# The second expert product as seven block products with transposed output, weights folded for four batches, and sums of weights kept in DRAM

## The chip, the cores and the metric

The kernel runs on one NeuronCore of a Trainium2 chip. The metric is the device time of one execution in microseconds. A core has TensorE (PE, with its weight loads as PEld), VectorE (DVE), ScalarE (ACT), GpSimd (POOL) and SyncE (SP), which issues the DMAs here. PE writes PSUM, which has eight banks of 512 float32 per partition; POOL works on SBUF alone.

## What is computed

Two attentions and a mixture of four experts (sizes: 8 batches, 8 heads, 576 tokens of 64; 32 packing queries; width 512, hidden width 1024):

```python
def sm_attn(qq, kk, vv):
    s = scale * np.matmul(qq, kk.transpose(0, 1, 3, 2))
    s = s - np.max(s, axis=-1, keepdims=True)
    a = np.exp(s)
    a = a / (np.sum(a, axis=-1, keepdims=True) + 1e-09)
    return np.matmul(a, vv)
p_packed = sm_attn(p, k, v)
out = sm_attn(q, p_packed, p_packed)
...
p = domain_probs / (domain_probs.sum(-1, keepdims=True) + 1e-09)
for e in range(E):
    h = np.maximum(x @ w1[e], 0.0)
    out += p[:, e:e + 1] * (h @ w2[e])
```

Here x holds the attention's output, one row for each of the 4608 tokens.

## The kernel before

**Folded first product.** The second attention's output is a product of token weights (32 per head) with packed values. So x @ w1 is computed as (token weights) @ (packed values @ w1). The inner factor is called G: for each head, 32 rows by the hidden width.

**Three products for one.** Operands of the large products are split into a high part, rounded to float32r, and a low part, the remainder. Each product is three TensorE products: high by low, high by high, low by high. `split` (L70 to L75) makes the parts: the high one with a cast, mostly on ACT, the low one with a subtraction, mostly on POOL.

**Tiling and loops.** Batches go in pairs: four superbatches of 1152 tokens. The hidden width of each expert is cut in two, so there are eight chunks (expert, half) for a superbatch, 32 in all. A chunk has these steps:
- `load_w1`, `load_w2`: loads 256 KB tiles (`wraw`) and splits them, anew for each superbatch.
- `g_stage` (L256): eight products of 512 columns, one for each head, for both batches; ACT copies the cross terms (L263), DVE adds them into `gs` (L265), ACT and DVE split the sum into `gh` and `gl`.
- `mm1` (L312): 16 groups of six products of 288 columns; the result has the hidden index on partitions and tokens along the free axis. ACT takes the relu as the high part (L316), DVE makes the low part (L317).
- `mm2` (L331): nine groups of twelve products of 512 columns, tokens on partitions. DVE multiplies by the expert's weight for each token and accumulates (L339; L336 for the first chunk). In the last chunk the accumulators go out (L342).

**Attention.** `pack_unit` is the first attention for one batch and four heads: scores (L113), softmax, transposes (L141, L145), packed values (L151, L159). `tok_unit` is the second attention's weights: scores (L182), 32 by 32 transposes and softmax on DVE (L186 to L198), split into `xh` and `xl`. Four units of each kind stand ahead of the loop, for the first superbatch, in an order that is written out by hand (the `emit` lines). The others are generators that advance by a stage at every second group of `mm2`.

**What sets the order.** The code is written in one order and the framework places the instructions of each engine, by its own model of time, where they can go; each engine then runs its list strictly in that order and waits at semaphores. All DMAs are issued from SP's list. Six PSUM banks serve `ps_aux`, two serve `ps_o`.

## Time and profile before

| | us |
|---|---|
| median of three runs | 1379.92 |
| range of the runs | 1378.01 to 1380.5 |
| span of the profiled execution | 1375.6 |

The profile is of one execution. Engine times in it are busy times; several engines are busy at once. A row of groups gives line, engine, operation, the tiles it writes and reads, shape, count, then busy time in us, mean ns of one, and the idle time of the engine ahead of them with what ended it. Products on PE overlap, so the mean of one is longer than the distance from one start to the next. A row of the chain or the timeline begins with the start and the length in us. Where groups of the same line have different shapes, the rows are shown by form.

The busiest groups on the engines other than PE are POOL's low parts of w1 (L75, 340.9 us in 252 instructions), DVE's additions into `gs` (L265, 338.1 us in 496) and DVE's low parts of the hidden values (L317, 216.7 us in 504).

### The profile page before, as it was taken

Reading aid. Unit: us, or ns where it says so; the run is one execution under the profiler, and the core shown is the slowest. Engines: PE = TensorE matmul, PEld = TensorE weight load, DVE = VectorE, ACT = ScalarE, POOL = GpSimd, SP = SyncE. Lnnn points to the kernel's source line nnn. Section 1 sums busy time; section 2 is a strip of 40 time slices with the busy share of each in tenths; the row PEclk is TensorE's granted clock in tenths of the full one; section 3 lists DMA queues with packets and bytes.
Section 4 is the critical chain, followed back from the end, with each engine's and each line's share of the span. In section 5 each row is a group of like instructions: output and inputs, shape, how many; then the busy total and the mean of one; then the engine's idle time right before and its main releaser. Section 6 shows DMA issues by size and latency. Waiting matters only on the chain.

```text
span 1375.6 us, 21317 instructions
## 1 busy us (share of the span) xinstructions
PE 1346.0 (98%) x7800; PEld 1144.1 (83%) x7800; DVE 993.8 (72%) x1734; ACT 690.8 (50%) x1402; POOL 568.9 (41%) x512
## 2 busy tenths in 40 slices
PE   6799999999999999999999999999999999999998
PEld 3588888878888888887888888888888888888887
DVE  7777766788867767689776667778867776666773
ACT  4744454545545545454555455554555455545531
POOL 4643444534434524444433445344444333443410
PEclk9899999999999999999999999999999999999999
DMA  9312222322232222222133222121123121112101
GB/s 296 105 40 80 74 87 72 98 66 85 73 114 83 80 76 71 88 72 65 55 100 102 84 77 82 56 88 55 54 62 108 47 61 55 54 55 62 54 1 69
DMA packets 64184, 106.83 MB, mean 78 GB/s; under 512 B 6097, under 2 KB 24657, under 8 KB 64081
## 3 DMA queue, kind: packets, MB, share of 16 engines
q1 hardware_dynamic: 64080, 105.48, 25.2%
q8 instruction: 62, 1.02, 0.3%
q14 instruction: 42, 0.34, 0.1%
HBM read 96.02 MB, written 9.44 MB: 77 GB/s over the span
## 4 chain that ended last, share of the span: by engine, by line
PE 86%; DVE 8%; POOL 2%; DMA 2%; issue 1%; ACT 1%; SPq 0%; POOLq 0%; ACTq 0%; DVEq 0%
PE ops L331 51%; PE aux L312 29%; PE aux L256 4%; DVE gs L265 3%; DMA wraw<-in_w 1%; DVE acc L339 1%; POOL w1st L75 1%; DVE gl L75 1%; PE aux L113 1%; DVE a L186 1%; PE aux L151 1%; DVE m L188 1%; DVE a L189 1%; PE aux L141 0%; DMA pb<-in_dp 0%
## 5 line engine op out<-in xcount | busy, mean ns | idle before, releaser
L75 POOL TENSOR_TENSOR w1st<-wraw,w1st 64x512 fp32r<-64x512 f32 x252 | 340.9, 1353 | 665.1 <-ACT w1st L72 626.7
L331 PE MATMUL ops<-w2l,hh 128*128 128x512 f32 x1152 | 450.9, 393 | 5.6 <-DVE acc L339 5.1
L331 PE MATMUL ops<-w2h,hh 128*128 128x512 f32 x1152 | 450.5, 391 | 0.0
L331 PE MATMUL ops<-w2h,hl 128*128 128x512 f32 x1152 | 448.1, 391 | 0.0
L265 DVE TENSOR_TENSOR gs<-aux,cross 32x512 f32<-32x512 f32 x496 | 338.1, 682 | 31.5 <-ACT cross L263 18.3
L317 DVE SCALAR_TENSOR_TENSOR hl<-aux,hh 128x288 fp32r<-128x288 f32 x504 | 216.7, 454 | 151.8 <-ACT hh L316 151.6
L312 PE MATMUL aux<-xl,gh 128*128 128x288 f32 x1008 | 295.7, 297 | 3.0 <-POOL xl L75 2.7
L312 PE MATMUL aux<-xh,gh 128*128 128x288 f32 x1008 | 295.2, 296 | 0.0
L339 DVE SCALAR_TENSOR_TENSOR acc<-ops,pb,acc 128x512 f32<-128x512 f32 x252 | 187.8, 749 | 137.3 <-PE ops L331 133.6
L312 PE MATMUL aux<-xh,gl 128*128 128x288 f32 x1008 | 284.1, 296 | 0.0
L316 ACT ACTIVATE hh<-aux 128x288 fp32r<-128x288 f32 x504 | 192.3, 414 | 171.8 <-PE aux L312 166.9
L331 PEld LDWEIGHTS ops<-w2l,hh 128*128 128x128 f32 x1152 | 216.3, 188 | 49.5 <-DVE acc L339 6.9
L263 ACT COPY cross<-aux 64x512 f32<-64x512 f32 x248 | 142.7, 582 | 225.5 <-PE aux L256 107.8
L331 PEld LDWEIGHTS ops<-w2h,hl 128*128 128x128 f32 x1152 | 215.6, 188 | 45.4
L331 PEld LDWEIGHTS ops<-w2h,hh 128*128 128x128 f32 x1152 | 216.2, 188 | 40.9
L72 ACT CAST w1st<-wraw 64x512 fp32r<-64x512 f32 x256 | 158.3, 618 | 143.9 <-DMA wraw<-in_w 140.1
L312 PEld LDWEIGHTS aux<-xl,gh 128*128 128x128 f32 x1008 | 190.0, 189 | 10.2 <-POOL xl L75 3.0
L312 PEld LDWEIGHTS aux<-xh,gh 128*128 128x128 f32 x1008 | 190.0, 189 | 5.0
L312 PEld LDWEIGHTS aux<-xh,gl 128*128 128x128 f32 x1008 | 187.3, 188 | 3.4
L75 POOL TENSOR_TENSOR w2l<-wraw,w2h 128x512 fp32r<-128x512 f32 x124 | 157.3, 1299 | 62.3 <-ACT w2h L72 39.0
L75 DVE TENSOR_TENSOR gl<-gs,gh 128x512 fp32r<-128x512 f32 x124 | 100.2, 829 | 19.9 <-ACT gh L72 19.4
L72 ACT CAST w2h<-wraw 128x512 fp32r<-128x512 f32 x128 | 78.1, 630 | 27.1 <-PE ops L331 6.5
(74 smaller groups left out, 675.7 us busy)
## 6 DMA issues: line engine op xcount, KB each, us to landing
wraw<-in_w SPq DMA_DIRECT2D x256, 256.0 KB, 2.9
kt<-in_k SPq DMA_DIRECT2D x32, 288.0 KB, 3.3
kt<-in_q SPq DMA_DIRECT2D x16, 576.0 KB, 3.8
out<-acc SPq DMA_DIRECT2D x36, 256.0 KB, 2.0
vt<-in_v SPq DMA_DIRECT2D x16, 512.0 KB, 4.7
vt<-in_v SPq DMA_DIRECT2D x16, 64.0 KB, 4.4
pt<-in_p SPq DMA_DIRECT2D x8, 64.0 KB, 3.4
pb<-in_dp SPq DMA_DIRECT2D x1, 72.0 KB, 5.7
```

What stands on the lines that cost most here:

```text
L72: nc.scalar.copy(out=dst_hi, in_=src)
L75: lo_eng.tensor_tensor(out=dst_lo, in0=src, in1=dst_hi.bitcast(F32), op=ALU.subtract)
L113: nc.tensor.matmul(out=ps[j * 64:(j + 1) * 64, 0:HS], lhsT=pbd[bi][:, 2 * g + j, :], rhs=kt[:, j, c * HS:(c + 1) * HS], start=True, stop=True,
L151: nc.tensor.matmul(out=ps[h * NPK:(h + 1) * NPK, 0:D], lhsT=at[0:n, c, h * NPK:(h + 1) * NPK], rhs=vt[0:n, c, h * D:(h + 1) * D], start=c ...
L256: nc.tensor.matmul(out=ps, lhsT=st["pgs"][:, h // 2, h % 2].rearrange("p a n -> p (a n)"), rhs=wst[h], start=True, stop=True,)
L263: nc.scalar.copy(out=cross, in_=ps[64:P, :])
L265: nc.vector.tensor_tensor(out=gs[hs * NPK:(hs + 1) * NPK, bi, :], in0=ps[bi * NPK:(bi + 1) * NPK, :], in1=cross[bi * NPK:(bi + 1) * NPK, : ...
L312: nc.tensor.matmul(out=ps, lhsT=lw[:, bi, g, fs], rhs=rx[:, g, ts], start=n == 0, stop=n == 3 * NG - 1)
L316: nc.scalar.activation(out=hh[:, ts], in_=ps, func=AF.Relu)
L317: nc.vector.scalar_tensor_tensor(out=hl[:, ts], in0=ps, scalar=0.0, in1=hh[:, ts].bitcast(F32), op0=ALU.max, op1=ALU.subtract)
L331: nc.tensor.matmul(out=ps, lhsT=lx[:, ts], rhs=rw, start=n == 0, stop=n == 3 * NFT - 1)
L339: nc.vector.scalar_tensor_tensor(out=acc, in0=ps, scalar=sc, in1=acc, op0=ALU.mult, op1=ALU.add)
```

## The change

- **Second product.** The work unit is one batch and one chunk (64 units). The hidden block of a unit is cut into 2 by 2 blocks (two halves of the tokens, 288 each, by two halves of the chunk's hidden width, 256 each), w2 into 2 by 2 blocks of 256 by 256. Strassen's scheme in Winograd's form makes seven block products of the blocks and their sums in place of eight. The operands in the order of `ORDER`: a11, s3, s1, s2, a22, s4, a12. The result has the output index on partitions and tokens along the free axis (288 columns a product); `finish` combines the seven accumulators once for a batch and stores the transposed output, which the host turns back.
- **The expert's weight** is multiplied into the hidden block when DVE drains `mm1_group` (relu and weight in one instruction), with the weights spread over all partitions from DRAM (`load_probs`).
- **Operands** are formed by `s_operand`: DVE makes the sum, ACT the high part, POOL the low part, two products ahead in the code (`LA = 2`).
- **Weight sums.** `t_form` makes the seven operands of a chunk from w2 in the first quarter: POOL makes four sums, ACT the high parts, POOL the low parts, and all go to DRAM (`td`). In the other three quarters `t_load` reads them back.
- **G for four batches.** `pga` and `pgb` hold four batches; two products a head give G for four of them, which ACT copies and four DMAs store to DRAM (`gd`); `g_load` reads a unit's part back, ACT and POOL split it. This runs in the first and third quarter, two chunks ahead. The low parts of w1 are DVE's in the first quarter, POOL's later.
- **Start.** Eight pack units (four batches) stand ahead of the loop instead of four. PSUM: two single banks (`aux`) and three pairs (`dbl`), which serve block products, `mm1_group`, and the attention's scores.
- **Attention**: the packed values come out transposed without a further transposition; softmax normalisation moves ahead of it.

The core of the diff, added lines (the lines that go are in the functions above):

```diff
+ORDER = ["a11", "s3", "s1", "s2", "a22", "s4", "a12"]
+NPROD = len(ORDER)
...
+    ps_aux = pool("ps_aux", 2, space=PSUM)
+    ps_dbl = pool("ps_dbl", 3, space=PSUM)
+    pga = const.tile([P, NPAIR, 2, P], F32R, name="pga")
+    pgb = const.tile([P, NPAIR, 2, P], F32R, name="pgb")
+    gd = [[dram.tile([HALF, H * NPK, FC], F32, name=f"gd{hf}_{c}") for c in range(NCH)] for hf in range(2)]
+    td = [[dram.tile([P, 2 * 2 * DH], F32, name=f"td{c}_{i}") for i in range(NPROD)] for c in range(NCH)]
+    pnd = dram.tile([E, NTOK], F32, name="pnd")
...
+    def g_heads(half, ch, lo_eng):
+        for h, wst in enumerate(w1_tiles(ch, lo_eng)):
+            yield
+            ps = aux()
+            nc.tensor.matmul(out=ps, lhsT=pga[:, h // 2, h % 2, :], rhs=wst, start=True, stop=False)
+            nc.tensor.matmul(out=ps, lhsT=pgb[:, h // 2, h % 2, :], rhs=wst, start=False, stop=True)
+            graw = gpool.tile([P, FC], F32, name="graw", bufs=2)
+            nc.scalar.copy(out=graw, in_=ps)
+            for bl in range(HALF):
+                nc.sync.dma_start(
+                    out=gd[half][ch][bl, h * NPK:(h + 1) * NPK, :], in_=graw[bl * NPK:(bl + 1) * NPK, :]
+                )
+            yield
+    units = [(sb, ch, 2 * sb + i) for sb in range(SB) for ch in range(NCH) for i in range(2)]
+    gs = {}
+    def g_load(u):
+        sb, ch, b = units[u]
+        gs[u] = []
+        for g in range(NG):
+            gk = gpool.tile([P, FC], F32, name="gk", bufs=2)
+            bl = b % HALF
+            nc.sync.dma_start(
+                out=gk,
+                in_=gd[b // HALF][ch][bl, g * P:(g + 1) * P, :],
+            )
+            ghl = gpool.tile([P, 2, FC], F32R, name="ghl", bufs=4)
+            hi_of(ghl[:, 0, :], gk, nc.scalar)
+            lo_of(ghl[:, 1, :], gk, ghl[:, 0, :], nc.gpsimd)
+            gs[u].append(ghl)
+            yield
+    pbt = {}
+    def load_probs(b, e):
+        t = wpool.tile([P, S], F32, name="pbt", bufs=3)
+        nc.sync.dma_start(out=t, in_=pnd[e:e + 1, b * S:(b + 1) * S].partition_broadcast(P))
+        pbt[b] = t
+    blocks = {}
+    def mm1_group(u, kh, c):
+        sb, ch, b = units[u]
+        xh, xl = xs[b]
+        ts = slice(c * HS, (c + 1) * HS)
+        ps = dbl()
+        for fi in range(2):
+            f = 2 * kh + fi
+            fs = slice(f * P, (f + 1) * P)
+            n = 0
+            for g in range(NG):
+                ghl = gs[u][g]
+                for hl, rx in ((0, xl), (0, xh), (1, xh)):
+                    nc.tensor.matmul(
+                        out=ps[:, fi, 0:HS], lhsT=ghl[:, hl, fs], rhs=rx[:, g, ts],
+                        start=n == 0, stop=n == 3 * NG - 1,
+                    )
+                    n += 1
+        a = hpool.tile([P, 2, HS], F32, name="ablk", bufs=6)
+        nc.vector.scalar_tensor_tensor(
+            out=a, in0=ps[:, :, 0:HS], scalar=0.0,
+            in1=pbt[b][:, ts].rearrange("p (o t) -> p o t", o=1).broadcast_to([P, 2, HS]),
+            op0=ALU.max, op1=ALU.mult,
+        )
+        blocks[u, f"a{c + 1}{kh + 1}"] = a
+    def s_operand(u, i):
+        name = ORDER[i]
+        blk = lambda n: blocks[u, n]
+        if name[0] == "s":
+            t = hpool.tile([P, 2, HS], F32, name="sblk", bufs=3)
+            x, y, op = {
+                "s1": ("a21", "a22", ALU.add), "s2": ("s1", "a11", ALU.subtract),
+                "s3": ("a11", "a21", ALU.subtract), "s4": ("a12", "s2", ALU.subtract),
+            }[name]
+            nc.vector.tensor_tensor(out=t, in0=blk(x), in1=blk(y), op=op)
+            blocks[u, name] = t
+        src = blk(name)
+        st = hpool.tile([P, 2, 2, HS], F32R, name="st", bufs=4)
+        hi_of(st[:, 0], src, nc.scalar)
+        lo_of(st[:, 1], src, st[:, 0], nc.gpsimd)
+        blocks[u, "op", i] = st
+    tt = {}
+    def t_load(ch, i):
+        t = wpool.tile([P, 2, 2, DH], F32R, name="tt", bufs=8)
+        nc.sync.dma_start(out=t.rearrange("p h f d -> p (h f d)").bitcast(F32), in_=td[ch][i])
+        tt[ch, i] = t
+    def t_form(ch):
+        e, hf = divmod(ch, F // FC)
+        raw = []
+        for kh in range(2):
+            r0 = hf * FC + kh * 2 * P
+            r = att.tile([P, 2, DM], F32, name=("kt", "vt")[kh])
+            nc.sync.dma_start(out=r, in_=w2[e, r0:r0 + 2 * P, :].rearrange("(f p) d -> p f d", p=P))
+            raw.append(r)
+        blk = {
+            "b11": raw[0][:, :, 0:DH], "b12": raw[0][:, :, DH:DM],
+            "b21": raw[1][:, :, 0:DH], "b22": raw[1][:, :, DH:DM],
+        }
+        yield
+        of = {"a11": "b11", "a12": "b21", "s4": "b22", "a22": "t4", "s1": "t1", "s2": "t2", "s3": "t3"}
+        how = {"t1": ("b12", "b11"), "t2": ("b22", "t1"), "t3": ("b22", "b12"), "t4": ("t2", "b21")}
+        for i, name in enumerate(ORDER):
+            n = of[name]
+            if n in how:
+                t = att.tile([P, 2, DH], F32, name={"t1": "at", "t2": "a1", "t3": "a1", "t4": "at"}[n])
+                nc.gpsimd.tensor_tensor(out=t, in0=blk[how[n][0]], in1=blk[how[n][1]], op=ALU.subtract)
+                blk[n] = t
+            t = wpool.tile([P, 2, 2, DH], F32R, name="tt", bufs=8)
+            hi_of(t[:, 0], blk[n], nc.scalar)
+            lo_of(t[:, 1], blk[n], t[:, 0], nc.gpsimd)
+            nc.sync.dma_start(out=td[ch][i], in_=t.rearrange("p h f d -> p (h f d)").bitcast(F32))
+            tt[ch, i] = t
+            yield
+    accs = {}
+    def product(u, i):
+        sb, ch, b = units[u]
+        st, t = blocks.pop((u, "op", i)), tt[ch, i]
+        ps = dbl()
+        for j in range(2):
+            n = 0
+            for fi in range(2):
+                for tl, sl in ((0, 1), (0, 0), (1, 0)):
+                    nc.tensor.matmul(
+                        out=ps[:, j, 0:HS], lhsT=t[:, tl, fi, j * P:(j + 1) * P], rhs=st[:, sl, fi, :],
+                        start=n == 0, stop=n == 5,
+                    )
+                    n += 1
+        if ch == 0:
+            accs[b, i] = apool.tile([P, 2, HS], F32, name=f"acc{i}")
+            nc.scalar.copy(out=accs[b, i], in_=ps[:, :, 0:HS])
+        else:
+            nc.vector.tensor_tensor(out=accs[b, i], in0=ps[:, :, 0:HS], in1=accs[b, i], op=ALU.add)
+    def finish(b):
+        m = {n: accs[b, i] for i, n in enumerate(ORDER)}
+        def store(t, r, n):
+            nc.sync.dma_start(
+                out=out[n * DH:(n + 1) * DH, b * S + r * HS:b * S + (r + 1) * HS].rearrange("(j p) t -> p j t", p=P),
+                in_=t,
+            )
+        def comb(dst, x, y, op=ALU.add):
+            nc.vector.tensor_tensor(out=dst, in0=x, in1=y, op=op)
+        comb(m["a12"], m["a11"], m["a12"])
+        store(m["a12"], 0, 0)
+        comb(m["s2"], m["a11"], m["s2"])
+        comb(m["s3"], m["s2"], m["s3"])
+        comb(m["s2"], m["s2"], m["s1"])
+        comb(m["s4"], m["s2"], m["s4"])
+        store(m["s4"], 0, 1)
+        comb(m["a22"], m["s3"], m["a22"], ALU.subtract)
+        store(m["a22"], 1, 0)
+        comb(m["s1"], m["s3"], m["s1"])
+        store(m["s1"], 1, 1)
...
+        drain(wavefront([pack_unit(b, g, unit_tile(2 * b + g)) for b in range(HALF) for g in range(NG)], 1))
+        norm_probs()
+        drain(g_heads(0, 0, nc.vector))
+        drain(wavefront([tok_unit(0, g) for g in range(NG)], 1))
+        drain(t_form(0))
+        for b in range(2):
+            load_probs(b, 0)
+        drain(g_load(0))
+        drain(wavefront([tok_unit(1, g) for g in range(NG)], 1))
+        drain(g_load(1))
+    hpool = ctx.enter_context(tc.tile_pool(name="hpool", bufs=1, reuse_waits="tile"))
+    apool = ctx.enter_context(tc.tile_pool(name="apool", bufs=2, reuse_waits="tile"))
+    def att_tile(shape, name):
+        return att.tile(shape, F32, name=name)
+    for kh, c in ((0, 0), (0, 1), (1, 1), (1, 0)):
+        mm1_group(0, kh, c)
+    LA = 2
+    for i in range(LA):
+        s_operand(0, i)
+    nothing = iter(())
+    back, gsteps, tsteps = nothing, nothing, nothing
+    GROUPS = {1: (0, 0), 3: (0, 1), 4: (1, 1), 6: (1, 0)}
+    for u, (sb, ch, b) in enumerate(units):
+        last_of_chunk = b % 2 == 1
+        nxt = units[u + 1] if u + 1 < len(units) else None
+        if not last_of_chunk:
+            if ch == 0 and sb % 2 == 1 and sb + 1 < SB:
+                back = chain(*[pack_unit(x, g, att_tile) for x in range(HALF, B) for g in range(NG)])
+            if ch == 5 and sb + 1 < SB:
+                back = chain(back, *[tok_unit(2 * sb + 2, g) for g in range(NG)])
...
+        if u == 0:
+            gsteps = g_heads(0, 1, nc.vector)
+        elif last_of_chunk:
+            nsb, nch = (sb, ch + 2) if ch + 2 < NCH else (sb + 1, ch + 2 - NCH)
+            gsteps = nothing
+            if nsb < SB and (nsb % 2 == 0):
+                if nch == 0:
+                    drain(back)
+                gsteps = g_heads(nsb // 2, nch, nc.vector if nsb == 0 else nc.gpsimd)
+        forming = last_of_chunk and sb == 0 and ch + 1 < NCH
+        if forming:
+            tsteps = t_form(ch + 1)
+            next(tsteps)
+        gl = g_load(u + 2) if u + 2 < len(units) else nothing
+        for i in range(NPROD):
+            product(u, i)
+            n = i + LA
+            if n < NPROD:
+                s_operand(u, n)
+            elif nxt:
+                s_operand(u + 1, n - NPROD)
+            for _ in range(1 if last_of_chunk else 4 if u == 0 else 2):
+                next(gsteps, None)
+            if nxt and i in GROUPS:
+                mm1_group(u + 1, *GROUPS[i])
+            if i in (4, 6):
+                if i == 4 and u + 2 < len(units) and units[u + 2][1] % 2 == 0:
+                    load_probs(units[u + 2][2], units[u + 2][1] // 2)
+                if i == 4 and not last_of_chunk:
+                    drain(gsteps)
+                next(gl, None)
+            if not forming:
+                next(back, None)
+            if last_of_chunk and nxt:
+                if forming:
+                    next(tsteps, None)
+                else:
+                    t_load(nxt[1], i)
+        if ch == NCH - 1:
+            finish(b)
+            if not last_of_chunk and sb + 1 < SB:
+                back = chain(back, *[tok_unit(2 * sb + 3, g) for g in range(NG)])
+            if last_of_chunk:
+                drain(back)
+                back = nothing
+        "dp": np.ascontiguousarray(np.asarray(moe_domain_probs).reshape(P, TP, E).transpose(0, 2, 1)),
...
+    out = nc.dram_tensor("out", (DM, B * S), F32, kind="ExternalOutput").ap()
+    return np.ascontiguousarray(r.results[0]["out"].T)
```

More of the change, by code (lines that the diff above doesn't have):

```diff
@@ L14 @@
 PSUM = bass.MemoryType.PSUM
+DRAM = bass.MemoryType.DRAM
 P = 128
@@ L147, in pack_unit @@
         yield
[L148 to L150 removed]
+        ps = aux()
+        for j in range(2):
+            for c, (_, n) in enumerate(SC):
                 nc.tensor.matmul(
[L152 to L155 removed]
```

404 lines of the change are left out of this document (112 added, 292 removed).

## Prediction

> **What bounds the kernel now.** I read the page's head and its chain of waits first, then the pieces of that chain in order of time, then the windows of a late stage and of the start.
>
> ```profile
> span 1375.6 us, 21317 instructions
> PE 1346.0 (98%) x7800; PEld 1144.1 (83%) x7800; DVE 993.8 (72%) x1734; ACT 690.8 (50%) x1402; POOL 568.9 (41%) x512
> PE 86%; DVE 8%; POOL 2%; DMA 2%; issue 1%; ACT 1%; SPq 0%; POOLq 0%; ACTq 0%; DVEq 0%
> ```
>
> PE holds 86% of the chain and is busy 98% of the span. Busy PE isn't PE at its peak, so the next thing is the spacing of its products, from pieces of the chain (start, length, count), and one window of the last quarter (columns: length, PE, PEld, DVE, ACT, POOL busy, clock, DMA share, GB/s).
>
> ```profile
> 271.16 7.17 PE aux L312 x54
> 1079.03 5.49 PE ops L331 x24
> 1118.37 5.49 PE ops L331 x24
> 1079.00:1118.00 39.00, 39.00 (x213) 34.21 (x212) 26.42 (x46) 20.08 (x41) 15.79 (x12) 1.00 0.19 55
> ```
>
> First products (L312, 288 columns) start every 7.17/54 = 0.1328 us, second ones (L331, 512 columns) every 5.49/24 = 0.2288. A chunk has 96 + 108 of them and 8 of L256, also 512 wide: 12.75 + 24.7 + 1.83 = 39.28 us. The same piece returns after 1118.37 - 1079.03 = 39.34. So a steady chunk is PE's issue rate and nothing else, and the other four engines have room (POOL 15.8 of 39).
>
> The ends, from the order of time and the windows:
>
> ```profile
> 36.00 0.27 PE L159 MATMUL aux<-ident,ppn 128*64 128x128 f32 x1
> 67.50 1.10 PE L256 MATMUL aux<-w1st,pgs 128*128 128x512 f32 x4
> 1371.76 0.75 DVE L339 SCALAR_TENSOR_TENSOR acc<-ops,pb,acc 128x512 f32<-128x512 f32 x1 [1.97 <-PE ops L331]
> 0.00:20.00 20.00, 10.71 (x118) 5.37 (x120) 11.91 (x36) 8.97 (x20) 7.44 (x13) 0.97 0.94 305
> 20.00:40.00 20.00, 16.36 (x153) 8.47 (x150) 18.88 (x45) 12.76 (x28) 13.91 (x26) 0.86 0.77 247
> 80.00:1040.00 960.00, 14.29 (x96) 5.82 (x96) 1.00 0.25 77
> ```
>
> The first chunk's first products end at 67.5, so the loop starts in effect at 67.5 - 12.75 = 54.7 us. The end after PE is 1375.6 - 1371.8 = 3.8. Then 1375.6 - 54.7 - 32 x 39.3 - 3.8 = 60 us are left for the attention inside the loop: 12 pack units and 12 token units, 5.0 a pair. The last row is L113 alone (the scores of 12 pack units; L182, the token units', gives the same row): 1.19 each. So a token unit is 1.2 on PE and a pack unit, waits included, 3.8.
>
> **The change on PE.** 32 x 108 = 3456 products of 512 columns become 64 units x 7 x 12 = 5376 of 288: 790.6 us become 713.9, **-76.7**. The seven products save an eighth; the narrower form gives back part, as 0.1328/288 is more per column than 0.2288/512. The Trainium skill, "TensorE: Matmul & The Clock Gate", Part 2, gives N/2.4 + 2.5 ns for a warm matmul; by it the two would be 746 and 658, -87. The rows here are some 10 ns longer at both widths, and I keep them. First products stay 3072. The G products stay 256 (two 512-wide ones a head, for four batches at once instead of one for two).
>
> A unit is 132 x 0.1328 = 17.5 us. By quarter (16 units, 280.5): the first adds 14 chunk-halves of G (7 x 3.66 = 25.6) and four token units (4.8): **311**. The second adds eight packs (30.4), four token units and two chunks of G (7.3): **323**. The third adds six chunks of G and four token units: **307**. The last has nothing: **280.5**. Sum 1221.5.
>
> **The start** grows: four more pack units stand ahead of G, and G goes out to DRAM and back. The loads of eight packs are 8 x 1.18 = 9.4 MB, 31 us at the 305 GB/s of the first window and 38 at the second's 247; in the run before, the last of four packs ended at 36.0, some 12 us after its loads (24 us at these rates for the 6.9 MB ahead of it). So the packs end at about 44 to 50. Behind them heads 4 to 7 have 16 stores.
>
> ```profile
> 22.64 0.53 SPq L89 DMA_DIRECT2D pt<-in_p  x1
> 1372.54 0.33 SPq L342 DMA_DIRECT2D out<-acc  x1
> wraw<-in_w SPq DMA_DIRECT2D x256, 256.0 KB, 2.9
> out<-acc SPq DMA_DIRECT2D x36, 256.0 KB, 2.0
> ```
>
> At 0.33 to 0.53 of SP each they take about 6.4, a store lands in 2.0, the load back in 2.9, and the split is 1.9 (0.69 + 1.25, rows below): 13 to 14 in all. The first product stands at 58 if nothing else is loaded ahead, at 72 if w1, w2 and q (3.3 MB) come first and the slower rate holds. I take **64**, 9 more than before. The end gets one combination more: 5.
>
> **POOL is the new bound to check.** It makes the low half of each operand. Rows (POOL alone; two and four at a stretch; then with a DVE instruction among them):
>
> ```profile
> 33.67 1.42 POOL L75 TENSOR_TENSOR xl<-a2t,xh 128x576 fp32r<-128x576 f32 x1 [3.72 <-ACT xh L72]
> 1101.06 5.05 POOL L75 TENSOR_TENSOR w2l<-wraw,w2h 128x512 fp32r<-128x512 f32 x4 [1.40 <-issue]
> 1097.02 2.64 POOL L75 TENSOR_TENSOR w1st<-wraw,w1st 64x512 fp32r<-64x512 f32 x2 [3.77 <-ACT w1st L72]
> 920.02 3.04 POOL L75 TENSOR_TENSOR w1st<-wraw,w1st 64x512 fp32r<-64x512 f32 x2 [4.24 <-ACT w1st L72]
> 920.55 1.38 DVE L189 TENSOR_TENSOR a<-a,m 128x576 f32<-128x576 f32 x1
> 1085.40 0.69 DVE L75 TENSOR_TENSOR gl<-gs,gh 128x512 fp32r<-128x512 f32 x1 [1.23 <-ACT gh L72]
> ```
>
> 576 elements take 1.42 (1.38 from start to start), 512 take 1.25. The fourth and fifth row show the two engines in each other's way: DVE's instruction with both inputs in SBUF came into a pair of POOL's, took 1.38, where one alone takes about 0.7, and the pair took 3.04 instead of 2.64. I charge POOL 0.40 for each.
>
> POOL in a chunk of the first quarter (two units): 14 low halves of operands x 1.38 = 19.3, 4 of G x 1.25 = 5.0, the w2 sums and their low halves (t_form, 11 x 1.25) 13.8, and 16 DVE instructions of the kind (8 operand sums, 8 w1 low halves) x 0.40 = 6.4: **44.5 against 38.7 of PE**. Seven such chunks, one without t_form (35.1, PE's) and four token units (1.38 and two DVE instructions of the kind each, 8.7): 355 against 311, **+44**. In the third quarter w1's low halves go to POOL (8 x 1.34): 19.3 + 5.0 + 10.7 + 3.2 = 38.2 against 38.7, level. In the second and last it is 27.5 against 35.1, hidden.
>
> What else lies beside:
>
> ```profile
> L265 DVE TENSOR_TENSOR gs<-aux,cross 32x512 f32<-32x512 f32 x496 | 338.1, 682 | 31.5 <-ACT cross L263 18.3
> L339 DVE SCALAR_TENSOR_TENSOR acc<-ops,pb,acc 128x512 f32<-128x512 f32 x252 | 187.8, 749 | 137.3 <-PE ops L331 133.6
> L189 DVE TENSOR_TENSOR a<-a,m 128x576 f32<-128x576 f32 x16 | 18.0, 1122 | 0.2
> L75 POOL TENSOR_TENSOR xl<-a2t,xh 128x576 fp32r<-128x576 f32 x16 | 23.9, 1491 | 31.9 <-ACT xh L72 31.8
> L72 ACT CAST xh<-a2t 128x576 fp32r<-128x576 f32 x16 | 11.1, 692 | 27.0 <-DVE a2t L198 27.0
> ```
>
> DVE in that chunk: 14 accumulations and 8 relu-and-weight steps from PSUM, scaled from 512 to 576 columns (0.75, 0.83), 16 contended ones at 1.12: 35, under POOL's 44.5. ACT: 14 x 0.69 and 27 of 512 columns, 0.62 by the same scale: 26. The DVE work that goes (L265 and the low halves of the hidden values) and ACT's relu pay for nothing, since both engines had room. DMA: 7 x 0.52 MB of sums, 1.05 of G and 0.3 of weights a chunk in 35 us, 143 GB/s where 305 was reached; the loads are issued a unit before their use. SP issues some 50 in a first-quarter chunk, 20 us of 44; behind a store that waits stand the G loads of two units on, which have a unit to spare. I cost these at nothing; without that cover see the fourth rival.
>
> **The sum.** 64 + 1221.5 + 5 = 1290.5; POOL +44; and 20 for hand-overs that can't be perfect (6 where POOL rules, 6 where POOL and PE are level, 8 for finish, whose bursts of seven DVE combinations, 7 x 1.12 = 8 us, PE has PSUM buffers for only in part; no row prices these, 0 to 40). That is 1354.5 in the span; the median of the runs stands 1379.9 - 1375.6 = 4.3 above its profile: **1358 us**.
>
> **Rivals.**
> - **PE rules everywhere.** If POOL's surplus drains into the free time of other units and DVE's sums fall into its gaps: 1290.5 + 14 + 4.3 = 1309. For it: POOL idled 60% before. Against: POOL's own work alone, 38.1 of the 44.5, is level with PE in the first quarter, t_form must be done there, and the sixteen DVE instructions come on top.
> - **The operands come late** (the slower side). s3, s1 and s2 each need DVE, ACT, then POOL: 1.12 + 0.69 + 1.49 = 3.30 us. If DVE takes a sum only behind the drain of the product two ahead, PE has two groups in that time, 2 x 12 x 0.1328 = 3.19, less the drain 0.75: 2.44. Each such sum costs 0.86, 41 us over the 48 units of the last three quarters for one a unit: 1399. It decides from 0.7 of a sum a unit on. Against: four operand buffers let ACT, POOL and DVE run further ahead if the order on DVE allows, and blocks are made up to eight groups before their use.
> - **A DVE instruction takes its whole length from POOL**, 0.69 in place of 0.40: 16 x 0.29 x 7 = +32, 1390. The Trainium skill, "SBUF — State Buffer", Who interferes with whom, has it so: two SBUF inputs on DVE against a GpSimd read is an exclusive lock, the loser blocked. That DVE waited (1.38 for 0.7) agrees; the 0.40 of the pair speaks for less.
> - **DRAM trips that aren't hidden**: 1 us at each of 25 chunk changes, 1383. Against: the DMA share and the unit of lead.
>
> That the change doesn't save the products is no case: the counts are fixed by the loops.
>
> **Numbers.** Within 0.2%, about what a measurement of this kernel can tell, is 1377.2 to 1382.7. Forecast 0.52 (1330 to 1385: 0.46 faster, 0.03 the same, 0.03 slower); PE alone 0.18, faster; late operands 0.20, slower; the whole lock 0.05, slower; DRAM 0.05 (0.01 the same, 0.04 slower). Faster 0.64, same 0.04, slower 0.32. The range 1310 to 1405 reaches both main rivals; below it lies half of the first, above it half of the second.
>
> **What would show it.** Spacing of the new products at 0.133; a late chunk without G of 35.1; POOL over 90% busy and PE waiting for POOL's low halves in the first quarter, chunk about 44 to 46, and hardly any such waits later; the first L312-like product at 64. Wrong if PE's waits for operands run through all quarters, if the first quarter keeps PE's 38.7, or if the start goes beyond 75.

## The result, and the profile after

The changed kernel takes **1469.2 us** (median of four runs, 1465.7 to 1475.3) where the kernel before takes 1379.0 on the same chip: ratio 1.066, interval 1.063 to 1.069. The forecast was 1358, and the time lies outside the range. The page's head, its engine line and its chain of waits:

```profile
span 1468.0 us, 25795 instructions
PE 1347.4 (92%) x9360; PEld 1267.2 (86%) x9360; DVE 1014.3 (69%) x1289; ACT 618.7 (42%) x1042; POOL 1168.0 (80%) x864
PE 56%; POOL 15%; DVE 12%; DMA 7%; issue 6%; SPq 2%; ACT 2%; DVEq 0%; POOLq 0%; ACTq 0%
```

POOL went from 41% to 80% of the span and PE's share of the chain from 86% to 56%. The windows show where. They are cut at the first block product of the units 0, 16, 32 and 48 (a unit issues 84 of them); columns as before: length, then busy time of PE, PEld, DVE, ACT, POOL. The last two rows are a quiet stretch and a quarter's end.

```profile
0.00:110.70 110.70, 81.67 (x364) 56.05 (x364) 55.96 (x116) 39.59 (x77) 51.38 (x90) 0.69 0.68 222
110.70:491.30 380.60, 333.46 (x2253) 313.34 (x2253) 301.50 (x322) 190.55 (x325) 353.48 (x227) 0.96 0.59 195
491.30:879.90 388.60, 365.05 (x2536) 338.33 (x2537) 249.95 (x333) 184.27 (x323) 326.88 (x260) 0.99 0.63 201
879.90:1178.40 298.50, 288.68 (x2144) 283.36 (x2145) 214.65 (x277) 105.59 (x167) 226.45 (x148) 1.00 0.46 152
1178.40:1460.80 282.40, 278.31 (x2066) 276.11 (x2064) 188.63 (x240) 98.67 (x154) 209.82 (x139) 0.99 0.38 127
960.00:1000.00 40.00, 40.00 (x303) 40.00 (x302) 24.80 (x34) 13.17 (x21) 31.34 (x22) 1.00 0.43 139
1152.60:1201.60 49.00, 41.34 (x283) 37.73 (x282) 43.86 (x53) 17.74 (x29) 33.23 (x20) 0.97 0.48 157
```

The prediction's terms put into the same cuts (the first block product stands one unit's first products, 48 x 0.1328 = 6.4 us, behind its start of 64; 6 of the allowance in the first quarter and 6 in the third, the 8 for `finish` shared among the three ends; the last quarter without the 6.4):

| stretch | predicted | measured | difference |
|---|---|---|---|
| to the first block product | 70.4 | 110.7 | +40.3 |
| first quarter | 363.7 | 380.6 | +16.9 |
| second | 325.7 | 388.6 | +62.9 |
| third | 315.7 | 298.5 | -17.2 |
| last | 274.1 | 282.4 | +8.3 |
| end | 5.0 | 7.2 | +2.2 |
| span | 1354.6 | 1468.0 | +113.4 |

The quiet stretch holds 303 products in 40.00 us, 0.132 each: the spacing that PE's saving of 76.7 rests on. From one unit's first block product to the next one's, 27 of 31 units in the last two quarters take 17.6 to 18.0 us. The time is lost in the start and in the first half. What PE waited for in the first quarter (in all, times, longest):

```profile
PE dbl L363 <- POOL st L90: 26.1, 13, 3.9
PE dbl L363 <- DVE acc L372: 14.2, 10, 2.9
```

And POOL's low halves of the operands, two groups of the first quarter and then one of the last:

```profile
L90 POOL TENSOR_TENSOR st<-sblk,st 128x576 fp32r<-128x576 f32 x65 | 107.2, 1657 | 16.2 <-ACT st L85 14.6 <-PE aux L237 1.5
L90 POOL TENSOR_TENSOR st<-ablk,st 128x576 fp32r<-128x576 f32 x48 | 81.3, 1702 | 0.2
...
L90 POOL TENSOR_TENSOR st<-sblk,st 128x576 fp32r<-128x576 f32 x63 | 96.8, 1545 | 57.4 <-ACT st L85 55.8 <-PE dbl L363 1.5
```

What took 1.42 alone in the kernel before takes 1.66 to 1.70 here. The single instructions show what goes with it: of the 113 in the first quarter, the 25 that overlap no DVE instruction with two SBUF inputs take 1.42 on average, the 88 that do take 1.75. Of the second quarter, the view of one tile tells what runs there on PE (`aux`, columns: min, median, max in ns, first and last start):

```profile
L159 PE MATMUL aux<-at,vt x160: 218/275/323, 509.0 to 616.4; 128*128 128x64 f32 x128, 64*128 64x64 f32 x32
L236 PE MATMUL aux<-w1st,pga x64: 390/398/505, 620.1 to 858.9; 128*128 128x512 f32 x64
```

64 products of L236 are the eight heads of all eight chunks: the whole of G for the last four batches runs between 620 and 859. The code of two of these chunks stands in the second quarter, that of the other six in the third; the same view of the third quarter has no G product at all. So the third quarter is shorter than predicted, and the second pays.

### The profile page after: what moved, and what is told of

It reads as the page before. It is cut to its first block, busy times and chain, and to the rows that moved or that the text cites. A ratio compares the mean times of both kernels' runs of the same rounds, so it can differ in the third digit from the quotient of the medians.

```text
span 1468.0 us, 25795 instructions
## 1 busy us (share of the span) xinstructions
PE 1347.4 (92%) x9360; PEld 1267.2 (86%) x9360; DVE 1014.3 (69%) x1289; ACT 618.7 (42%) x1042; POOL 1168.0 (80%) x864
## 4 chain that ended last, share of the span: by engine, by line
PE 56%; POOL 15%; DVE 12%; DMA 7%; issue 6%; SPq 2%; ACT 2%; DVEq 0%; POOLq 0%; ACTq 0%
PE dbl L363 31%; PE dbl L286 18%; POOL st L90 6%; DMA gd<-graw 4%; PE aux L159 3%; DVE acc L384 3%; POOL ghl L90 3%; POOL tt L90 3%; DVE sblk L309 2%; DVE w1st L227 2%; DVE acc L372 2%; SPq L241 2%; DVE ablk L292 2%; POOL w1st L227 1%; PE dbl L128 1%
## 5 line engine op out<-in xcount | busy, mean ns | idle before, releaser
L363 PE MATMUL dbl<-st,tt 128*128 128x288 f32 x5376 | 786.0, 299 | 66.4 <-POOL st L90 38.3
L363 PEld LDWEIGHTS dbl<-st,tt 128*128 128x128 f32 x5376 | 741.9, 190 | 96.1 <-POOL st L90 51.2
L90 POOL TENSOR_TENSOR st<-sblk,st 128x576 fp32r<-128x576 f32 x256 | 401.4, 1575 | 157.8 <-ACT st L85 145.8
L286 PE MATMUL dbl<-xh,ghl 128*128 128x288 f32 x2048 | 423.5, 299 | 0.0
L372 DVE TENSOR_TENSOR acc<-dbl,acc 128x576 f32<-128x576 f32 x392 | 293.9, 752 | 140.7 <-PE dbl L363 139.7
L286 PEld LDWEIGHTS dbl<-xh,ghl 128*128 128x128 f32 x2048 | 336.3, 192 | 1.1
L90 POOL TENSOR_TENSOR st<-ablk,st 128x576 fp32r<-128x576 f32 x192 | 298.1, 1557 | 33.4 <-ACT st L85 30.5
L286 PE MATMUL dbl<-xl,ghl 128*128 128x288 f32 x1024 | 308.5, 301 | 9.3 <-ACT ghl L85 2.6
L286 PEld LDWEIGHTS dbl<-xl,ghl 128*128 128x128 f32 x1024 | 197.2, 193 | 13.7 <-ACT ghl L85 3.6
L227 POOL TENSOR_TENSOR w1st<-wraw,w1st 64x512 fp32r<-64x512 f32 x64 | 94.8, 1482 | 6.1 <-ACT w1st L85 1.3
L236 PE MATMUL aux<-w1st,pga 128*128 128x512 f32 x128 | 56.8, 444 | 20.8 <-ACT graw L239 15.3
```

The lines of the kernel that those rows point to most:

```text
L90: eng.tensor_tensor(out=dst, in0=src, in1=hi.bitcast(F32), op=ALU.subtract)
L227: lo_eng.tensor_tensor(out=wst[other, :], in0=raw[rows, :], in1=wst[rows, :].bitcast(F32), op=ALU.subtract)
L236: nc.tensor.matmul(out=ps, lhsT=pga[:, h // 2, h % 2, :], rhs=wst, start=True, stop=False)
L286: nc.tensor.matmul(out=ps[:, fi, 0:HS], lhsT=ghl[:, hl, fs], rhs=rx[:, g, ts], start=n == 0, stop=n == 3 * NG - 1,)
L363: nc.tensor.matmul(out=ps[:, j, 0:HS], lhsT=t[:, tl, fi, j * P:(j + 1) * P], rhs=st[:, sl, fi, :], start=n == 0, stop=n == 5,)
L372: nc.vector.tensor_tensor(out=accs[b, i], in0=ps[:, :, 0:HS], in1=accs[b, i], op=ALU.add)
```

## The experiments

All runs were timed against the kernel before. Ratios with their intervals; the stretches are cut as above, at the exact starts, so they can differ by 0.1 from the windows.

| run | us | ratio | first block product | quarters |
|---|---|---|---|---|
| changed kernel | 1469.2 | 1.066 [1.063, 1.069] | 110.7 | 380.5, 388.7, 298.5, 282.4 |
| e1_packed_rows | 1452.1 | 1.055 [1.053, 1.056] | 107.7 | 377.3, 376.0, 298.5, 282.4 |
| e2_no_t_low | 1422.2 | 1.032 [1.031, 1.034] | 109.9 | 333.4, 387.2, 300.2, 282.3 |
| e3_g_held | 1457.4 | 1.058 [1.056, 1.060] | 108.1 | 379.3, 343.2, 333.3, 282.4 |
| e4_w1_low_dve | 1467.7 | 1.065 [1.063, 1.066] | 108.4 | 380.0, 389.2, 297.8, 282.3 |
| e5_t_form_later | 1450.8 | 1.052 [1.051, 1.054] | 94.2 | 391.7, 375.8, 298.5, 282.4 |
| e6_tok_early | 1460.1 | 1.059 [1.057, 1.062] | 109.8 | 379.0, 384.2, 294.9, 279.1 |
| e7_sums_dve | 1458.6 | 1.058 [1.057, 1.060] | 109.9 | 368.9, 386.8, 298.9, 282.4 |
| e8_four_edits | 1430.5 | 1.038 [1.036, 1.040] | 94.1 | 387.9, 328.1, 332.0, 279.1 |
| e9_no_t_low_later | 1400.6 | 1.015 [1.014, 1.017] | 93.7 | 339.5, 377.7, 298.5, 282.4 |
| e10_finish_split | 1428.8 | 1.036 [1.034, 1.038] | 96.6 | 388.8, 324.6, 331.1, 278.7 |
| e11_full_rows | 1403.5 | 1.018 [1.016, 1.020] | 91.4 | 365.0, 326.4, 329.5, 279.1 |
| e12_all | 1405.4 | 1.019 [1.017, 1.022] | 94.6 | 366.2, 323.8, 331.6, 278.4 |
| e13_one_store | 1466.0 | 1.063 [1.061, 1.064] | 102.1 | 384.2, 387.5, 300.3, 282.4 |
| e14_one_store_all | 1474.5 | 1.069 [1.067, 1.071] | 98.0 | 390.2, 327.4, 371.3, 279.1 |
| e15_three_ahead | 1474.3 | 1.068 [1.067, 1.070] | 95.7 | 392.4, 327.5, 366.3, 279.1 |
| e16_store_act | 1442.1 | 1.046 [1.044, 1.048] | 106.6 | 372.1, 372.8, 299.0, 282.4 |
| e17_store_act_all | 1411.6 | 1.024 [1.022, 1.026] | 104.7 | 361.8, 327.9, 328.0, 279.1 |

How far such a stretch moves by itself can be read off the table: e3, e4, e6 and e7 leave the code of the start alone, and their first block products stand at 108.1 to 109.9 against 110.7; e3 and e4 leave the first quarter alone too, and it ends at 487.4 and 488.4 there against 491.3. A difference of 3 or 4 us in these two places tells nothing.

**Which engine holds the first quarter.** The low parts of the weight sums go from POOL to ACT. They become copies of the high parts, so this kernel leaves low by high out and adds high by high twice; the number of PE's products stays:

```diff
-            lo_of(t[:, 1], blk[n], t[:, 0], nc.gpsimd)
+            hi_of(t[:, 1], blk[n], nc.scalar)
```

> The low parts of the weight sums are copies of the high parts, made by ACT, so POOL has 49 subtractions less in the first quarter; the low-by-high term is left out of the computation in this way. Theory (POOL, with the DVE instructions in its way, sets the first quarter): 49 x 1.53 = 75 us less POOL, first quarter from 380.5 to 315-330 where PE takes over, total about 1400-1415. Rival (the latency of the chain DVE, ACT, POOL sets it, not POOL's sum of work): first quarter above 360, total above 1445.

The quarter fell by 47, to 333.4, and the other stretches moved by less than 2. That is a little above the theory's 315 to 330, and far from the rival's 360. Its window:

```profile
109.90:443.20 333.30, 316.87 (x2244) 301.10 (x2245) 278.05 (x318) 208.29 (x365) 282.86 (x178) 1.00 0.68 221
```

POOL did 71 us less; PE now is busy for 317 of 333. So POOL's amount of work did hold the quarter. With it gone the quarter is 16 us longer than PE's busy time.

**Can DVE take it?** In e7 three of the four weight sums go to DVE, from the second chunk on; in e4 the low parts of w1 for the last four batches do, which are made in the second quarter:

```diff
-                nc.gpsimd.tensor_tensor(out=t, in0=blk[how[n][0]], ...
+                (nc.gpsimd if n == "t4" or ch == 0 else nc.vector).tensor_tensor(
```

> Against the changed kernel (first quarter 380.5, GpSimd busy 354 of it, VectorE 311): three of the four weight sums of a chunk go from GpSimd to VectorE, from the second chunk on, 21 operations in all. Theory A (GpSimd is the bound of the first quarter by its amount of work, VectorE has room): first quarter 345 to 360, time 1440 to 1450. Theory B (the two engines hinder each other, so that work moved between them gains little, as when the low parts of w1 were moved in the second quarter): first quarter 372 to 385, time 1460 to 1472.

```diff
-                gsteps = g_heads(nsb // 2, nch, nc.vector if nsb == 0 else nc.gpsimd)
+                gsteps = g_heads(nsb // 2, nch, nc.vector)
```

> The low parts of w1 for the second half of the batches are made by DVE, as in the first half. Theory (POOL's load sets the units with G of the second quarter, 64 subtractions of 1.48 there): POOL -95 +25 us for DVE in its way, second quarter from 388.7 to 360-370, total 1440-1450. Rival (DVE becomes the bound, or PE is it already): second quarter within 8 us, total 1460-1480.

Their windows of the quarter in question, e7's first, then e4's second:

```profile
109.90:478.80 368.90, 328.02 (x2252) 310.04 (x2253) 324.23 (x342) 189.50 (x323) 334.59 (x207) 0.98 0.61 202
```

```profile
488.40:877.60 389.20, 363.94 (x2536) 337.52 (x2537) 300.50 (x393) 184.60 (x323) 248.78 (x200) 0.99 0.65 202
```

e7 lies between its theories: POOL lost 19 us of work, DVE gained 23, the quarter became 11.6 shorter. In e4 POOL lost 78 and DVE gained 51, and the quarter didn't move: what PE waited longest for there turned from POOL's `st` (9.6) to DVE's accumulation:

```profile
PE dbl L363 <- DVE acc L372: 7.8, 10, 1.9
PE dbl L363 <- POOL st L90: 4.8, 2, 3.0
```

My theory for e4 fell. The run doesn't tell the two halves of its rival apart: DVE took over the waits, but PE was busy for 364 of 389 before and after, so little could be gained there from POOL at all. What the second quarter pays for is PE's own work, as e3 and e1 show. That POOL's work costs about as much on DVE rests on e7, where both were busy, and not on e4.

**G ahead of its quarter.** In e3 each G product of the last four batches has to stand, on PE, behind the block product at which it is written:

```diff
+            with tc.issue_after(anchor[0].ins) if half == 1 else ExitStack():
+                nc.tensor.matmul(out=ps, lhsT=pga[:, h // 2, h % 2, :], rhs=wst, start=True, stop=False)
...
+                    anchor[:] = [nc.tensor.matmul(
```

> The G products of the third quarter are queued on PE behind the block product that stands before them in the code, so they can't move ahead into the second quarter. Theory (they were moved ahead, into a quarter where PE had the pack units and POOL was full, and away from one with room): second quarter from 388.7 to 345-355, third from 298.5 to 315-325, total 1445-1455. Rival (the second quarter's length is its own work): second quarter within 10 us, third longer, total 1465-1490.

The windows of the second and third quarter:

```profile
487.40:830.60 343.20, 330.45 (x2431) 315.64 (x2432) 238.95 (x333) 128.60 (x221) 257.63 (x211) 1.00 0.53 168
830.60:1163.90 333.30, 316.85 (x2252) 304.33 (x2252) 239.26 (x277) 158.78 (x269) 296.63 (x197) 0.99 0.64 197
```

The second quarter became 45.5 shorter and the third 34.8 longer: G went where it was written. Both are somewhat past what the theory said. The whole is 12 shorter. A likely reason, not tested by itself, is that the third quarter had room on POOL (226 busy of 298 before this edit, in the windows above).

**Packed values and boundaries.** e1 puts the old form of the packed values back (weight loads of 32 columns, then a transposition); e6 writes the token scores of the second batch of the next pair in the last chunk's even unit instead of behind `finish`:

```diff
-                    out=ps[:, j * 64:(j + 1) * 64], lhsT=vt[0:n, c, j * P:(j + 1) * P],
-                    rhs=at[0:n, c, j * 64:(j + 1) * 64], ...
+                    out=ps[h * NPK:(h + 1) * NPK, 0:D], lhsT=at[0:n, c, h * NPK:(h + 1) * NPK],
+                    rhs=vt[0:n, c, h * D:(h + 1) * D], ...
```

> Packed values made in the old form (32-column weights, 64-column stream, then a transposition). Theory (the new form's 128-column weight loads in float32 cost PE 3.7 us a pack unit ahead of the loop and 2.8 in it, where the old form took 1.0): first block product from 110.7 to 90-97 us, second quarter from 388.7 to about 373, total about 1435-1442. Rival (loads, SP's order and the trip through DRAM set the start): the start stays within 5 us, total 1450-1458.

```diff
-            if ch == 7 and sb + 1 < SB and sb % 2 == 0:
-                pass
+            if ch == 7 and sb + 1 < SB:
+                back = chain(back, *[tok_unit(2 * sb + 3, g) for g in range(NG)])
```

> Against the changed kernel (1469.2; units on both sides of a quarter's end take 25.8 and 23.2 us instead of 17.6, three times): the token scores of the batch after next are issued one unit earlier, in the even unit of the last chunk, instead of behind the seven closing combinations of the first batch. Theory A (at the quarter's end VectorE has the token scores and the combinations at once): the pair of units falls from 49.0 to 40 to 44 at each of three ends, time 1447 to 1456. Theory B (the seven combinations and the sums of the operands alone fill VectorE there, wherever the token scores stand): no pair changes by over 2, time 1464 to 1471.

The groups of the packed values, in the changed kernel and in e1:

```profile
L159 PE MATMUL aux<-at,vt 128*128 128x64 f32 x256 | 39.6, 305 | 1.7 <-ACT at L150 1.7
L159 PE MATMUL aux<-at,vt 64*128 64x64 f32 x64 | 15.9, 333 | 0.0
```

```profile
L159 PE MATMUL aux<-vt,at 128*32 128x64 f32 x512 | 12.9, 251 | 1.9 <-ACT at L150 1.9
L159 PE MATMUL aux<-vt,at 64*32 64x64 f32 x128 | 6.1, 254 | 0.0
L166 PE MATMUL aux<-ident,ppn 128*64 128x128 f32 x16 | 5.0, 310 | 5.3 <-DVE ppn L164 4.0 <-DVE rs L143 1.2
```

55.5 us for 16 pack units against 24.0 with twice the products and the transposition: 2.0 a unit more. The eight units of the second quarter by themselves take 23.8 against 10.3 (the same groups, between 491 and 640), and the quarter gave back 12.7 of these 13.5. At the start the saving of 18 brought the first block product from 110.7 to 107.7, which is no more than it moves by itself, so the rival was right about the start, and its range holds the time too. In e6 the three units around each quarter's end fell by 5.2, 5.2 and 1.5, nine in the whole: the time lies between the two theories, and the gain is least where only `finish` and the operands' sums are left. Giving three of the seven combinations to POOL (e10, on top of e8) gained 1.7, within the intervals:

> On top of e8_four_edits (1430.5; its two later quarter's ends take 27.5+25.2+19.9 and 22.1+24.7+19.9 us where three units of the quiet stretches take 52.8 to 59.8): three of the seven closing combinations of batches 2 to 7 go from VectorE to GpSimd. Theory A (VectorE's work at the quarter's end is the cause): each of these two ends is shorter by 4 to 7, the first (batches 0 and 1, left as it is) is not; time 1416 to 1424. Theory B (a combination on GpSimd hinders VectorE as long as it saves it): each end within 2, time 1427 to 1434.

The third quarter, in e8 and then in e10:

```profile
810.10:1142.20 332.10, 318.48 (x2251) 306.05 (x2251) 238.42 (x276) 159.38 (x269) 297.68 (x197) 0.99 0.63 197
810.00:1141.10 331.10, 316.35 (x2252) 304.49 (x2252) 235.66 (x271) 160.15 (x270) 313.30 (x208) 0.99 0.64 201
```

The window 1152.6 to 1201.6 of the changed kernel had shown DVE busy for 43.9 of 49. In e10 DVE has 3 us less in the quarter and POOL 16 more, and the three units around the ends of the second and third quarter take 74.1 instead of 72.6 and 64.4 instead of 66.7. Theory A fell.

**The start.** e5 (on top of e1) moves the first chunk's weight sums behind the first loads of G; e9 adds e2's edit:

```diff
-        drain(t_form(0))
...
         drain(g_load(1))
+        drain(t_form(0))
```

> On top of e1_packed_rows (1452.1, first group of first products at 94.7, first product at 107.7): the first chunk's weight sums are issued behind the first two folded-weight loads, so that GpSimd reaches the copies of the last packed values before them. Theory A (the start is late because those copies stand behind the weight sums on GpSimd, while TensorE lies almost idle from 57 to 94): folded weights from about 60, first group at 82 to 86, first product at 95 to 98, time 1438 to 1444. Theory B (the start is set by the trip of the folded weights to DRAM and back and by the head splits on ScalarE): first group stays at 93 to 96, and the weight sums are now late for the first product, time 1452 to 1460.

> The edits of e1_packed_rows, e2_no_t_low and e5_t_form_later together: the low parts of the weight sums are copies of their high parts on ScalarE, so the low-by-high term of the second products is left out, and GpSimd is off the bound of the first quarter. Theory A (the 13.5 us that e5 won at the start were given back because GpSimd's work up to the end of the first quarter is one sum that it has to get through, wherever the first product stands): here the gain stays; first product at 93 to 96, first quarter 330 to 340, time 1390 to 1400. Theory B (the later weight sums themselves hold the first products up): first quarter 345 to 352, time 1404 to 1412.

In e5 the first block product came 13.5 us earlier, even a little more than theory A had it, but the quarter became 14.4 longer: it ended at 485.9 against e1's 485.0, and the time of theory A was missed. The windows, e5's first, then e9's:

```profile
0.00:94.20 94.20, 58.64 (x536) 36.01 (x537) 58.88 (x127) 38.53 (x76) 40.07 (x83) 0.78 0.71 218
94.20:485.90 391.70, 335.88 (x2249) 314.58 (x2247) 307.37 (x319) 191.75 (x327) 365.63 (x235) 0.96 0.62 200
```

```profile
93.70:433.20 339.50, 320.09 (x2248) 304.93 (x2249) 284.16 (x318) 214.49 (x376) 289.14 (x180) 0.99 0.69 227
```

POOL's work up to the end of the first quarter is 40.1 + 365.6 = 405.7 in e5, 407.6 in e1 and 51.4 + 353.5 = 404.9 in the changed kernel: moving it didn't move the end. With POOL's load taken off (e9) the first block product comes 16.2 before e2's and the quarter ends 10.0 before e2's. The quarter, 339.5, is what theory A said, and the time of 1400.6 stands just above its range. But e9 holds e1's edit too, which alone went with an end 6.3 earlier (491.3 to 485.0), so how much of the earlier start stays by the move itself is open.

Then what holds the first block product? In e5 SyncE issues the 32 stores of the first chunk in a row, ahead of the first loads:

```profile
57.39 16.82 SPq L245 DMA_DIRECT2D gd<-graw  x32
74.25 0.93 SPq L259 DMA_DIRECT2D gk<-gd  x2
```

e13 stores a head at once (the G buffer ordered by head), e16 leaves the transfers and issues the stores from ACT:

```diff
-                    out=gd[half][ch][bl, h * NPK:(h + 1) * NPK, :], in_=graw[bl * NPK:(bl + 1) * NPK, :]
+            nc.sync.dma_start(out=gd[half][ch][h], in_=graw)
...
-                in_=gd[b // HALF][ch][bl, g * P:(g + 1) * P, :],
+                in_=gd[b // HALF][ch][4 * g:4 * g + 4, bl * NPK:(bl + 1) * NPK, :],
```

> On top of e5_t_form_later (1450.8; first group 77.6, first product 94.2, first quarter 391.7, ends at 485.9): the folded weights lie in DRAM by head, so that one store of 256 KB a head replaces four of 64 KB. Theory A (SyncE's queue holds the start: 32 stores in a row take it from 57.4 to 74.2, and the first loads back stand behind them): first group at 65 to 70, first product at 82 to 88; the end of the first quarter stays at 482 to 487, because it is set by GpSimd and VectorE; time 1443 to 1451. Theory B (the token chain of VectorE and ScalarE holds the start): first group stays at 75 to 78, time 1448 to 1453.

```diff
-                nc.sync.dma_start(
+                nc.scalar.dma_start(
                     out=gd[half][ch][bl, ...
```

> On top of e5_t_form_later (1450.8; first group 77.6, first product 94.2, first quarter ends at 485.9): the stores of the folded weights are issued by ScalarE, right behind its copy, instead of SyncE; four stores of 64 KB a head as before. Theory A (SyncE's 32 stores in a row, 16.8 us, hold the start): first group at 65 to 72, first product at 82 to 89, end of the first quarter at 480 to 487 all the same, time 1442 to 1451. Theory B (the token chain, or the trip itself, holds it): first group at 75 to 79, time 1448 to 1455. If issuing costs ScalarE time that is missed: above 1455.

e13 is no clean test: a load now gathers four pieces, and its trip (issue to the split on ACT) went from 74.25 to 76.93, 2.7 us, to

```profile
66.67 0.65 SPq L256 DMA_DIRECT2D gk<-gd  x1
```

```profile
72.36 0.62 ACT L85 CAST ghl<-gk 128x512 fp32r<-128x512 f32 x1 [2.91 <-DMA gk<-gd]
```

5.7 us, and PE's waits for `graw` in the whole rose from 14.6 to 34.3. Its first group came at 73.0 and its time at 1466.0, outside both theories. e16 leaves the transfers as they were: its first group starts at 76.2 against 77.6, so freeing SyncE's list of these stores gained 1.4 and not the 6 to 13 of theory A. What shows in its place is on ACT, whose copies out of PSUM wait for one of two `graw` buffers until the stores have landed:

```profile
62.85 0.58 ACT L243 COPY graw<-aux 128x512 f32<-128x512 f32 x1 [4.29 <-DMA gd<-graw]
...
74.56 0.59 ACT L243 COPY graw<-aux 128x512 f32<-128x512 f32 x1 [4.89 <-DMA gd<-graw]
```

But e16 isn't free of a cost of its own: behind its first group, PE's list holds G products of the next chunk, and they wait 14.6 us in three pieces for `graw`, while ACT stands 7.3 us before its next cast (at 90.6) with stores to issue. PE's waits for `graw` in the whole rose to 32.6 here too. With these waits the first block product comes 12.4 later than e5's. Yet e16 is 8.7 us faster than e5: its first quarter ends at 478.7, 7 earlier. Why is open; no run separates it. A third `graw` buffer wasn't tried.

**Less work for both engines.** e8 joins e1, e3, e5 and e6. It came out at 1430.5, where its expectation puts it if the third or the fourth edit gives nothing; its first quarter ends at 482.0. On top of it, e11 forms the low parts of w1 in the first half with one 128-row instruction for two heads in place of two of 64 rows, pays with a third G product a head, and gives the room to e7's sums:

```diff
+            if half == 0:
+                whi = wpool.tile([P, FC], F32R, name="w1st", bufs=4)
+                wlo = wpool.tile([P, FC], F32R, name="w1st", bufs=4)
+                hi_of(whi, raw, nc.scalar)
+                lo_of(wlo, raw, whi, lo_eng)
...
+                pairs = [(x[rows, h // 2, h % 2, :], w[rows, :]) for x, w in ((pga, wst[1]), (pga, wst[0]), (pgb, wst[0]))]
```

> The edits of e1_packed_rows, e3_g_held, e5_t_form_later and e6_tok_early together. If they act on separate stretches (loop of the second quarter -12.7 and start -3 by the first, -10.7 by the second, -11 by the third, -15 to -20 by the fourth): 1410 to 1425. If the third or the fourth gives nothing: 1425 to 1442. In no case below 1379, because the first quarter keeps its GpSimd work of 354 us.

> On top of e8_four_edits (first quarter 387.9 with GpSimd busy 379, VectorE 322, TensorE 334): in the first half the low parts of w1 are formed for two heads in one 128-row operation instead of one 64-row operation for each (32 operations of VectorE less in the first quarter, some 41 us at 1.29) and a folded weight takes three half-high products instead of two (64 x 0.229 = 14.6 us more on TensorE); the room goes to the sums t1 to t3, as in e7_sums_dve (GpSimd some 20 us less). Theory A (VectorE and GpSimd together bound the first quarter, so that work taken away from both shortens it): first quarter 350 to 368, time 1393 to 1411. Theory B (GpSimd's low parts alone, or TensorE's own waits, bound it): first quarter 375 to 390, time 1418 to 1433.

```profile
91.40:456.40 365.00, 347.34 (x2301) 312.92 (x2301) 299.03 (x316) 174.52 (x299) 337.17 (x215) 0.97 0.64 211
```

e11 took 27 us from e8, 22.9 of them in the first quarter: theory A, and the first quarter is now near PE (347 of 365). POOL and DVE together are busy for 636 us there where e8 has 681. How much of the gain is the full rows and how much e7's move, no run separates. Of the versions that leave nothing out it is the best, still 1.8% slower than the kernel before. Joining e10 and e11 (e12) gave nothing more; e13's layout on top of e11 (e14) cost 71, 25 in the first quarter and 42 in the third, as loads came late (ACT idle for `gk` 207 us in the whole against 59), and far outside both of its expectations, 1388 to 1406; three operands ahead instead of two (e15) changed nothing beside e14, so on that kernel the waits are not hand-overs that a longer lead cures; e16's move on top of e11 (e17) was 8 us slower, its first block product 13.3 later, and above the 1408 from which on its expectation has ACT missing the time for issuing.

## Why the prediction was wrong, point by point

- **PE's saving**: right. Spacing 0.132 against 0.1328; quiet units take 17.6 us against 17.5.
- **What failed**: the third quarter's six chunks of G ran in the second (e3: 45.5 there), a pack unit was taken over at its old price (e1: 12.7), and the start was put at 64 as a term of its own where the first product came at 98.3; each is told below. With the edits of e1, e3, e5 and e6 together (e8), 74 us of the 113 in the span are left: 48 by the end of the first quarter (482.0 against 434.1), 2.4 in the second, 16.3 in the third, 7.3 behind it. e11 takes the 48 down to 22. So the second quarter is accounted for, and the rest in part.
- **POOL in the first quarter**: the amount was right, 355 predicted for the stretch that POOL rules, 353.5 busy, 93% of the window, and PE's longest waits there are for it, as forecast. At 1.38 and 1.25 us each the 227 instructions of that window make 299; the other 54.7 over DVE's 137 instructions with two SBUF inputs are 0.40 each, the price that the prediction took from one pair. That the price fits is partly luck: a second such instruction ran beside most of the pair's second half, which ended at 923.06, and the prediction put the whole 0.40 on the first:

```profile
921.85 1.77 DVE L75 TENSOR_TENSOR gl<-gs,gh 128x512 fp32r<-128x512 f32 x1
```

  The rival of the whole length (0.69) and the rule of the Trainium skill behind it ("SBUF — State Buffer", Who interferes with whom: an exclusive lock, the loser blocked) would have given 393; measured is less. What failed here is the 6 us of hand-overs: POOL was idle for 27 of the 380.6.
- **The start**: the step "first product at 64" failed by 34, as the first group came at 98.3. The 48 products behind it took 12.4 instead of 6.4, 0.24 apart up to 108.3 and 0.13 after that, at a granted clock of 0.59 in this window; together that is the 40 of the table. Its "wrong if the start goes beyond 75" came true. The first link that failed is "the packs end at about 44 to 50": the last packed values start on PE at 68.5, though their loads had landed by 42.5, and at 56.2 with the old form (e1). Of the 40, e1 and e5 together took 16 away, nearly all of it once the order on POOL was changed (e5: 13.5); the G stage's two buffers, each tied to the landing of its stores, show in e16's waits, but no run freed them, so their share of the other 24 stays open. Adding the start to the first quarter as a term of its own failed too: 94.2 led to 485.9 in e5, 107.7 to 485.0 in e1, 106.6 to 478.7 in e16. POOL's t_form(0) and packing copies belong to the same sum as the first quarter, and the prediction counted only what stood inside it.
- **The second quarter**, the largest miss (+62.9), has three steps in it. "The third adds six chunks of G": the placement put all eight into the second (e3: 45.5 there, 34.8 given back in the third). A pack unit "3.8" on PE, taken over from the kernel before without pricing its new form: 1.7 more a unit in this quarter (e1: 12.7). The cover of the boundary: e6, 4.5. With these undone e8's second quarter is 328.1 against the 325.7 predicted. "In the second and last it is 27.5 against 35.1, hidden" held only for chunks without G and packing beside them: the units of the last quarter take 17.6, half of 35.2.
- **Quarter's ends**: of its own "0 to 40" the prediction took 8 for `finish`, which is too little. At the last end two units take 49.0 where two quiet ones take 35.2: 13.8, with DVE busy for 43.9 of the 49; 41 for all three, an estimate if the other two cost as much. Token units run there too: writing some of them a unit earlier (e6) took 12 of it over the three ends, the engine of the combinations (e10) next to nothing.
- **G in the third quarter**: held there, its units take 19.9 instead of 17.6, so 4.6 a chunk and not 3.66. That is 5.6 for the six chunks; e3's third quarter is 333.3 against 315.7, and the other 12 are not priced.
- **The rivals**: late operands in all quarters didn't happen, as most units of the last two run at PE's spacing; that PE rules everywhere didn't happen either. Trips through DRAM didn't cost at the chunk changes: ACT waited 6.2 us in all for loads of G in the changed kernel. The outcome was none of the four but several terms that were each too low, which the range didn't allow for. The sum itself has a slip of 1: 1354.5 + 4.3 is 1358.8.

## What to carry to other kernels

- Where one engine is full over several stages, add its work from the first instruction that can run to the end of the last stage; "start" and "first quarter" are then one term, and a run that only moves the start shows it.
- Where GpSimd and VectorE are both busy with sums of two SBUF operands, they lengthen each other's instructions, so moving a pass between them gains less than it takes away (11.6 of 19 in e7). Less work for both gained more: 23 of the first quarter in e11, whose edit uses all 128 rows and holds e7's move too.
- A framework that places instructions by its own model may move work of a later stage that has room into an earlier, full one; look where a group runs, and tie it if need be (e3).
- Taking work off an engine that isn't the limit gains nothing: e4 took 78 us off POOL in a quarter where PE was busy for 364 of 389. Read the busy time of the others first.

## What the runs showed of the hardware that was not expected

- A short float32 product costs more with a 128-column weight load than with one of 32 columns: 320 products of 64 columns took 55.5 us against 19.0 for 640 of the old form (rows above). Half of each stands in the start, where the granted clock was 0.69 in the changed kernel and 0.73 in e1; the half in the second quarter, at 0.99, took 23.8 for 160 against 8.0 for 320.
- A load of 256 KB that gathers four pieces of 64 KB took 5.7 us to its use, where one piece took 2.7 (one pair of rows at the start, with other transfers beside). In the whole, ACT was idle 23.7 us for such loads in e13 against 4.4 in e5; the stores had changed too, so the cause is not shown.
- DVE's sums of operands take longer where POOL is busy, as POOL's low halves do beside DVE. One group of them in the first and in the last quarter of the changed kernel:

```profile
L309 DVE TENSOR_TENSOR sblk<-ablk 128x576 f32<-128x576 f32 x33 | 41.4, 1255 | 2.8
L309 DVE TENSOR_TENSOR sblk<-ablk 128x576 f32<-128x576 f32 x30 | 26.3, 876 | 3.3 <-DVE ablk L292 0.5
```

1.26 us with POOL busy for 93% of the window, 0.88 with POOL busy for 74%.
